# Retention, gated and squared-ReLU feed-forward on one core: where the states are summed, when weight pieces come, and which places stay empty

## The chip, the core and the metric

The kernel runs on one core of one Trainium2 chip. The metric is the device time of one execution in microseconds (us); the median of the runs shown is compared. Engines are named as in the profile: PE (TensorE), DVE (VectorE), ACT (ScalarE), POOL (GpSimd), SP (the queue that issues every DMA here).

## The reference

```
# q, k, v: 4 batches, 8 heads, 576 positions, 64 wide; gamma_h = 1 - 2^(-5-h)
scores = q k^T / sqrt(64)
attn   = (scores * gamma_h^(i-j) where i >= j, else 0) v         # no softmax
x = attn as 2304 tokens x 512
xn = x / rms(x) * rms_g
y = ((silu(xn w_gate) * (xn w_val)) w_out)                        # 512 -> 1536 -> 512
out = (relu(y w_in)^2) w_out2                                     # 512 -> 2048 -> 512
```

All arrays are float32, and so is the result.

## The kernel before, in words

**Precision.** Each float32 operand of the two feed-forward layers is split into a high and a low part that PE takes as fp32r, and every product is three matmuls (high x high, high x low, low x high; `mm3`, L386 to L388). Weights come as 512 KB pieces (`load_piece`, L101, three buffers `st`) and are split on the chip by a "conversion" (`convert_piece`): three ACT instructions (L124, L125, L137) and four on DVE (L126, L129, L132, L138). After a conversion has been put in the program, `load_ahead` puts the load of a later piece into SP's queue; `cv["ahead"]` says how many pieces may be on their way. The load of piece i+3 must wait until piece i's buffer has been read for the last time (L132).

**Attention.** Two heads form a pair; there are 16 pairs, n = 0 to 15. The attention runs in chunks of 128 positions: scores inside a chunk (`scores`, L233), masked by DVE into `ret` (L243, and L251 for the last 64 positions), a running state per chunk (`state`: products k^T v on PE into the PSUM tile `u`, L262; then R by one ACT copy, L269, and a chain of three DVE instructions, L271), and `outputs` (L286 and L294 on PE, scaled by DVE into X, L298). The loop over n does, in this order on PE: `scores(n, 0)`, first place, `outputs(n-1, 0)`, `state(n)`, second place, `scores(n, 1)`, `outputs(n-1, 1)`.

**PSUM.** `bank2("A0")` and `bank2("A1")` are two-bank tiles, one buffer each: the first takes half 0 of a pair's scores (columns 0 to 255 of either bank, one bank a head), the second half 1. Tags "G" and "V" are single banks with two buffers each that go round. Up to pair 7 (`alone["on"]`) the state's `u` comes from "G"; from pair 8 on it comes from "V", which the two outputs of each pair use too, and also the two small matmul groups of the norm (`beside`: "roots", L356, and "scale", L363).

**The places.** From pair 8 on (`mixed`, FIRST = 7) the feed-forward of the first token tile is done beside the attention: 20 blocks (gate or value product of one of 10 column groups, 12 matmuls each) are spread by `block()` over NPOINT = 2 x 9 - SKIP places; with SKIP = 1 only the first place of pair 8 is empty. Each block calls `halves(1)`, and every second half allows one conversion; the end of a mixed pair allows another, and `CONVERT_ALONE` names the pairs before that allow one (2, 3 and 7). `CONVERT_BEHIND` and `cv["phase"]` keep the conversions of some phases behind the last DVE and ACT instructions written before them (phase 2 in pair 8, phase 1, without that, from pair 9).

**The norm.** `NORMS` says behind which half of which pair the squares, the roots, the scaling (L326) and the split into `xh` and `xl` (L373, L374) of a 256-token group stand; these are traced with high priority. Groups 0 and 1 make the first tile (512 tokens), group 2 the second tile (256 tokens), whose split (`split_x(off1[1], T1[1])`) stands behind the first tile's last block.

**Order.** PE and SP keep the order of the program (`manual_schedule`). The order on DVE, ACT and POOL is made by the framework's scheduler, which plays the program through with modelled durations and priorities. Every queue is in order on the chip.

The lines of the state before:

```
u = bank("G" if alone["on"] else "V", f"u{n}")
for c in range(4):
    for h in range(2):
        r = slice(h * D, h * D + D)
        nc.tensor.matmul(u[r, c * D:c * D + D], raw_k[n][:, c, r], vsc[n][:, c, r], start=True, stop=True)
```

Of the kernel before, what the change touches and what calls it, by code (L numbers as in the profile page):

```python
# [22 lines left out]
C = 128  # L23
# [5 lines left out]
T1 = [512, 256, 512, 512, 512]  # L29
# [5 lines left out]
ORDER = [*range(NBESIDE, NF1), *range(NBESIDE)]  # L35
NWA, NWC = NGV + NKEPT // 2, 1
NWB = NF1 - NKEPT // 2 - NWC
SKIP = 1
FIRST = 7
WARM = (8, 6, 5, 5)  # L40
WARM_PAIR = {1: (1, 1), 2: (1, 1)}
NORMS = {
    (4, 0): [("squares", 0)], (4, 1): [("squares", 1)], (5, 0): [("roots", 0)], (5, 1): [("roots", 1)],
    (6, 1): [("scale", 0), ("split", 0)], (7, 0): [("scale", 1), ("split", 1)],
    (9, 1): [("squares", 2)], (11, 0): [("roots", 2)], (12, 0): [("scale", 2)],
}
LOAD_W = (3,)
CONVERT_ALONE = {2: 2, 3: 2, 7: 2}
CONVERT_BEHIND = ("", "", "ad", "ad")
RSQRT_MAGIC = float(0x5F3759DF)  # L50
I32 = mybir.dt.int32
# [5 lines left out]
def retention_then_glu_then_relu2(ctx: ExitStack, tc: tile.TileContext, qk, kv, w1, w2, g, cmask, cvs, cgi, cgc, cid, out):  # L57
# [15 lines left out]
    def bank(tag, name):  # L73
        return psum.tile([P, 512], F32, tag=tag, name=name)

    def bank2(tag, name):
        return psum.tile([P, 2, 512], F32, tag=tag, name=name, bufs=1)
# [18 lines left out]
    def load_piece():  # L96
        i = cv["load"]
        if i >= cv["load_lim"]:
            return
        t = stage.tile([P, 512, 2], I32, tag="st", name=f"raw{i}")  # L100
        nc.sync.dma_start(out=t.rearrange("p n t -> p (n t)"), in_=src[i].bitcast(I32))  # L101
        raws[i] = t
        cv["load"] += 1

    def load_ahead(i):
        while cv["load"] < min(i + cv["ahead"], cv["load_lim"]):
            load_piece()
# [33 lines left out]
    def halves(k):  # L141
        cv["half"] += k
        while cv["half"] >= 2 and convert():
            cv["half"] -= 2
        cv["half"] = min(cv["half"], 2)

    def need(n):
        while cv["done"] < n:
            assert convert()
# [9 lines left out]
    alone = {"on": True}  # L159
    raw_qk, raw_k, vsc, rets, Rs = {}, {}, {}, {}, {}  # L160

    def load_qk(n, parts=(slice(0, S),)):
        if n >= NPAIR:
            return
        if n not in raw_qk:
            b, k = (B - 2 if n % 4 > 1 else B - 1), n % 2 * 2
            raw_qk[n] = ap.tile([P, 2, S], F32, tag="qk", name=f"qk{n}") if n > 9 and n % 4 > 1 else (
                X[:, k:k + 2, b * S:b * S + S]
            )
        for r in parts:  # L170
            nc.sync.dma_start(out=raw_qk[n][:, :, r], in_=qk[n][:, :, r])

    def load_kv(n):
        if n >= NPAIR:
            return
        if n > 1:
            raw_k[n] = kvp.tile([P, 4, P], F32, tag="k", name=f"k{n}")
            vsc[n] = ap.tile([P, 5, P], F32, tag="v", name=f"v{n}", bufs=4)
        else:
            t = X[:, 2 + n, :9 * P].rearrange("p (c n) -> p c n", c=9)  # L180
            raw_k[n], vsc[n] = t[:, :4], t[:, 4:]
        nc.sync.dma_start(out=raw_k[n], in_=kv[n][:, :4])
        nc.sync.dma_start(out=vsc[n], in_=kv[n][:, 4:])
# [5 lines left out]
    ret4 = [ap.tile([P, 2, REM], F32, tag=f"ret4{i}", name=f"ret4_{i}", bufs=1) for i in range(2)]  # L189
    for t in ret4:  # L190
        nc.gpsimd.memset(t[REM:], 0.0)
    junk = {}

    def keep_warm(k, new=False):
        if new:
            junk["t"] = bank("G", f"junk{len(junk)}")
        for _ in range(k):
            nc.tensor.matmul(junk["t"][:, :P], zero, zero, start=True, stop=True)
# [12 lines left out]
        nc.sync.dma_start(out=t, in_=a)  # L211
    for c0, w in ((C, C), (2 * C, REM)):
        nc.gpsimd.tensor_copy(gi[:, :, c0:c0 + w], gi[:, :, :w])
    for n in (2, 3):
        load_qk(n)
        load_kv(n)
        cv["ahead"] += 1
        load_ahead(0)

    def scale_v(n):  # L220
        if n >= NPAIR:
            return
        hp = n % HP
        for h in range(2):
            r = slice(h * D, h * D + D)
            last_on["a"] = nc.scalar.activation(
                out=vsc[n][:, :, r], in_=vsc[n][:, :, r], func=AF.Copy, scale=vs[:, 2 * hp + h:2 * hp + h + 1]
            )

    def score(dst, n, c, h, w):  # L230
        r = slice(h * D, h * D + D)
        cs = slice(c * C, c * C + w)
        nc.tensor.matmul(dst, raw_qk[n][r, 1, cs], raw_qk[n][r, 0, cs], start=True, stop=True)  # L233

    def scores(n, half):
        hp = n % HP
        ps = bank2("A0" if half else "A1", f"s{n}_{half}")
        for j in range(2 + half):
            w = REM if j == 2 else C
            for h in range(2):  # L240
                score(ps[:w, h, j * C:j * C + w], n, 2 * half + j, h, w)
        t = ap.tile([P, 2, 2 * C], F32, tag="ret", name=f"ret{n}_{half}", bufs=3)
        last_on["d"] = nc.vector.tensor_tensor(  # L243
            out=t.rearrange("p h (c i) -> p h c i", c=2),
            in0=ps[:, :, :2 * C].rearrange("p h (c i) -> p h c i", c=2),
            in1=mask[:, 2 * hp:2 * hp + 2, None, :].to_broadcast([P, 2, 2, C]),
            op=ALU.mult,
        )
        rets[n, half] = t
        if half:  # L250
            last_on["d"] = nc.vector.tensor_tensor(  # L251
                out=ret4[n % 2][:REM], in0=ps[:REM, :, 2 * C:2 * C + REM],
                in1=mask[:REM, 2 * hp:2 * hp + 2, :REM], op=ALU.mult,
            )

    def state(n):
        hp = n % HP
        u = bank("G" if alone["on"] else "V", f"u{n}")
        for c in range(4):
            for h in range(2):  # L260
                r = slice(h * D, h * D + D)
                nc.tensor.matmul(  # L262
                    u[r, c * D:c * D + D], raw_k[n][:, c, r], vsc[n][:, c, r],
                    start=True, stop=True,
                )
        if n > 1:
            load_kv(n + 2)
        R = ap.tile([P, 4, D], F32, tag="R", name=f"R{n}")
        last_on["a"] = nc.scalar.activation(out=R[:, 0], in_=u[:, 0:D], func=AF.Copy)  # L269
        for c in range(1, 4):  # L270
            last_on["d"] = nc.vector.scalar_tensor_tensor(  # L271
                out=R[:, c], in0=R[:, c - 1], scalar=gc[:, hp:hp + 1], in1=u[:, c * D:c * D + D],
                op0=ALU.mult, op1=ALU.add,
            )
        Rs[n] = R
# [94 lines left out]
    def split_x(tok, n, col0=0):  # L370
        for k in range(KC):
            src_, d = X[:, k, tok:tok + n], slice(col0, col0 + n)
            last_on["a"] = nc.scalar.activation(out=xh[:, k, d], in_=src_, func=AF.Copy)  # L373
            last_on["d"] = nc.vector.tensor_tensor(out=xl[:, k, d], in0=src_, in1=xh[:, k, d].bitcast(F32), op=ALU.subtract)  # L374


    off1 = [sum(T1[:i]) for i in range(len(T1))]
# [98 lines left out]
    blocks = [(kind, f) for f in range(NBESIDE) for kind in (glu_gate, glu_val)]  # L476
    NPOINT = 2 * (NPAIR - FIRST) - SKIP
    points = {"n": -SKIP, "done": 0}

    def block():  # L480
        points["n"] += 1
        while points["done"] < min(len(blocks), points["n"] * len(blocks) / NPOINT):
            i = points["done"]
            need(i + 1)
            blocks[i][0](0, blocks[i][1], "G")
            points["done"] += 1
            halves(1)

    def stages(n, half):
        with tc.high_priority():  # L490
            for what, i in NORMS.get((n, half), ()):
                beside(what, i)

    for n in range(1, NPAIR + 1):
        mixed = n > FIRST
        if n in LOAD_W:
            cv["ahead"] += 1
            load_ahead(cv["done"])
        if n == FIRST + 1:
            alone["on"] = False  # L500
            cv["phase"] = 2
        if n == FIRST + 2:
            cv["phase"] = 1
        if n < NPAIR:
            scores(n, 0)
        if mixed:
            block()
        else:
            keep_warm(WARM_PAIR.get(n, (0, 0))[0], n in WARM_PAIR)
        outputs(n - 1, 0)  # L510
        stages(n, 0)
        if n < NPAIR:
            state(n)
            if n == NPAIR - 1:
                att_kv.close()
                wpool["c"] = ctx.enter_context(tc.tile_pool(name="wc", bufs=NWC, side="right", reuse_waits="tile"))
                cv["lim"] = NGV + NWC
                cv["load_lim"] = NP1
                load_ahead(cv["done"])
        if mixed:  # L520
            block()
        else:
            keep_warm(WARM_PAIR.get(n, (0, 0))[1])
        if n < NPAIR:
            scores(n, 1)
        outputs(n - 1, 1)
        stages(n, 1)
        scale_v(n + 1)
        halves(CONVERT_ALONE[n] if n in CONVERT_ALONE else 2 * mixed)
    need(NGV)  # L530
# [12 lines left out]
    for f in range(NBESIDE, NF1):  # L543
# [2 lines left out]
        halves(1)  # L546
        glu_val(0, f, "G")
        halves(1)
    split_x(off1[1], T1[1])
    norms = iter(())  # L550
    LAG = 2
    for f in range(NF1 + LAG):
# [161 lines left out]
```

## Time and profile before

| | us |
|---|---|
| median of three runs | 952.05 (947.85 to 953.3) |
| profiled execution | 944.46 |
| its span (first to last instruction) | 942.7 |
| PE busy | 929.0 (99%) |
| DVE busy | 456.4 (48%) |
| ACT busy | 338.6 (36%) |
| granted PE clock, mean | 0.999 |

The attention and what runs beside it fill about the first 150 us; the rest is the feed-forward. A pair's instructions are found in the timeline by their order. A row of a timeline has the start, the time until the last one of the row ends, the engine, the line, the output and inputs, the count, and in brackets the idle time of the engine just before with what ended it.

### The profile page before, as it was taken

What the parts mean: (1) busy time and instruction counts of PE and PEld (TensorE: products, weight loads), DVE (VectorE), ACT (ScalarE), POOL (GpSimd) and SP (SyncE); (2) the same over time, 40 slices, a digit from 0 to 9 for tenths busy, and PEclk for the clock granted to TensorE, in tenths of its full rate; (3) what the DMA queues carried; (4) which work ended last, traced back from release to release, by engine and by line L of the source; (5) the groups of instructions that cost most, each with busy time, mean ns of one, the idle gap of its engine ahead of it and who ended that gap; (6) DMA issues with size and microseconds to landing.
All of it is one profiled execution on the core that took longest, in us unless ns stands there. A gap on an engine that the chain in (4) does not pass through costs nothing.

```text
span 942.7 us, 12628 instructions
## 1 busy us (share of the span) xinstructions
PE 929.0 (99%) x5228; PEld 776.3 (82%) x5228; DVE 456.4 (48%) x859; ACT 338.6 (36%) x606; POOL 22.5 (2%) x56
## 2 busy tenths in 40 slices
PE   9999999999999999999999999999999999999998
PEld 8777777999888888888888888888888888888897
DVE  4987794765644123512677776442223223322322
ACT  3564552652311121112555655432223222322332
POOL 0200000021100000000000000000000000000000
PEclk9999999999999999999999999999999999999999
DMA  9865641410000000100144422001001000100010
GB/s 326 301 218 188 230 162 46 136 44 1 1 1 23 0 1 1 39 7 0 67 134 134 135 89 90 1 5 41 0 1 45 1 1 1 45 1 1 1 46 23
DMA packets 22554, 60.92 MB, mean 65 GB/s; under 512 B 2656, under 2 KB 3936, under 8 KB 22496
## 3 DMA queue, kind: packets, MB, share of 16 engines
q1 hardware_dynamic: 22496, 60.11, 18.8%
q8 instruction: 41, 0.67, 0.3%
q14 instruction: 17, 0.14, 0.0%
HBM read 55.39 MB, written 4.72 MB: 64 GB/s over the span
## 4 chain that ended last, share of the span: by engine, by line
PE 89%; DMA 5%; DVE 3%; ACT 1%; issue 1%; SPq 1%; ACTq 0%
PE pr L388 7%; PE b L628 7%; PE pr L387 7%; PE pr L386 7%; PE b L629 7%; PE b L630 7%; PE a L387 5%; PE a L386 5%; PE a L388 5%; PE pg L386 5%; PE pg L387 5%; PE pg L388 5%; PE pv L386 5%; PE pv L388 5%; PE pv L387 5%; DMA raw<-in_w 4%
## 5 line engine op out<-in xcount | busy, mean ns | idle before, releaser
L617 DVE TENSOR_TENSOR X<-X 128x512 f32<-128x512 f32 (+1 forms) x80 | 51.1, 639 | 189.3 <-ACT X L616 188.6
L415 ACT ACTIVATE h<-X 128x512 fp32r<-128x512 f32 (+1 forms) x132 | 77.5, 587 | 161.7 <-DVE X L434 86.8
L416 DVE TENSOR_TENSOR h<-X,h 128x512 fp32r<-128x512 f32 (+1 forms) x132 | 84.5, 640 | 70.7 <-ACT h L415 69.5
L388 PE MATMUL pr<-xh,w 128*128 128x512 f32 (+1 forms) x320 | 117.7, 368 | 0.0
L387 PE MATMUL pr<-xl,w 128*128 128x512 f32 (+1 forms) x320 | 117.7, 368 | 0.0
L386 PE MATMUL pr<-xh,w 128*128 128x512 f32 (+1 forms) x320 | 117.6, 368 | 0.0
L616 ACT ACTIVATE X<-pr 128x512 f32<-128x512 f32 (+1 forms) x80 | 44.5, 556 | 194.5 <-PE pr L388 194.3
L628 PE MATMUL b<-w,h 128*128 128x512 f32 x288 | 112.4, 390 | 0.0
L629 PE MATMUL b<-w,h 128*128 128x512 f32 x288 | 112.2, 390 | 0.0
L630 PE MATMUL b<-w,h 128*128 128x512 f32 x288 | 112.0, 389 | 0.0
L386 PE MATMUL pv<-xh,w 128*128 128x512 f32 (+1 forms) x240 | 90.5, 377 | 0.0
L387 PE MATMUL pg<-xl,w 128*128 128x512 f32 (+1 forms) x240 | 88.6, 369 | 1.6 <-DVE xl L374 1.6
L386 PE MATMUL pg<-xh,w 128*128 128x512 f32 (+1 forms) x240 | 89.6, 373 | 0.0
L387 PE MATMUL a<-h,w 128*128 128x512 f32 (+1 forms) x240 | 88.5, 369 | 0.0
L386 PE MATMUL a<-h,w 128*128 128x512 f32 (+1 forms) x240 | 88.5, 369 | 0.0
L388 PE MATMUL pv<-xh,w 128*128 128x512 f32 (+1 forms) x240 | 88.4, 368 | 0.0
L388 PE MATMUL pg<-xh,w 128*128 128x512 f32 (+1 forms) x240 | 88.4, 368 | 0.0
L388 PE MATMUL a<-h,w 128*128 128x512 f32 (+1 forms) x240 | 88.4, 368 | 0.0
L387 PE MATMUL pv<-xl,w 128*128 128x512 f32 (+1 forms) x240 | 88.3, 368 | 0.0
L434 DVE TENSOR_TENSOR X<-pv,X 128x512 f32<-128x512 f32 (+1 forms) x52 | 32.7, 628 | 110.9 <-PE pv L388 109.1
L426 ACT ACTIVATE X<-pg 128x512 f32<-128x512 f32 (+1 forms) x52 | 28.5, 549 | 114.0 <-PE pg L388 114.0
L387 PEld LDWEIGHTS pr<-xl,w 128*128 128x128 f32 x320 | 60.3, 188 | 10.7
(93 smaller groups left out, 1412.0 us busy)
## 6 DMA issues: line engine op xcount, KB each, us to landing
raw<-in_w SPq DMA_DIRECT2D x68, 512.0 KB, 3.7
X<-in_qk SPq DMA_DIRECT2D x11, 576.0 KB, 6.2
out<-o SPq DMA_DIRECT2D x18, 256.0 KB, 2.1
v<-in_kv SPq DMA_DIRECT2D x14, 320.0 KB, 4.3
k<-in_kv SPq DMA_DIRECT2D x14, 256.0 KB, 3.1
qk<-in_qk SPq DMA_DIRECT2D x4, 576.0 KB, 4.2
X<-in_kv SPq DMA_DIRECT2D x2, 320.0 KB, 5.3
X<-in_kv SPq DMA_DIRECT2D x2, 256.0 KB, 5.0
```

Source lines behind the costliest of these rows:

```text
L386: nc.tensor.matmul(dst, whi, xhi, start=start, stop=False, skip_group_check=True)
L387: nc.tensor.matmul(dst, whi, xlo, start=False, stop=False, skip_group_check=True)
L388: nc.tensor.matmul(dst, wlo, xhi, start=False, stop=stop, skip_group_check=True)
L415: last_on["a"] = nc.scalar.activation(out=h[:, 0, :n], in_=s, func=AF.Copy)
L416: last_on["d"] = nc.vector.tensor_tensor(out=h[:, 1, :n], in0=s, in1=h[:, 0, :n].bitcast(F32), op=ALU.subtract)
L426: last_on["a"] = nc.scalar.activation(out=s, in_=pg[:, :n], func=AF.Silu)
L434: last_on["d"] = nc.vector.tensor_tensor(out=s, in0=pv[:, :n], in1=s, op=ALU.mult)
L616: last_on["a"] = nc.scalar.activation(out=s, in_=pg[:, :n], func=AF.Relu)
L617: last_on["d"] = nc.vector.tensor_tensor(out=s, in0=s, in1=s, op=ALU.mult)
L628: nc.tensor.matmul(a[m], hh, w[:, 0], start=f == 0, stop=False)
L629: nc.tensor.matmul(a[m], hh, w[:, 1], start=False, stop=False)
L630: nc.tensor.matmul(a[m], hl, w[:, 0], start=False, stop=f == NF2 - 1)
```

## The change

States: when `alone` is off, `state(n)` writes its 256 columns into columns 256 to 511 of the first bank of the pair's own half-0 scores tile (A0), where before it took a bank from "V". Prologue: `LOAD_W` is emptied, and three weight pieces are loaded before the loop, each ahead of the q, k and v of pairs 2 and 3 (the third behind them), where before there were two, each behind them. Pair 1 allows a conversion too. Both places of pair 8 are empty, so 20 blocks are spread over 16 places. Roots and scaling of group 2 stand one half and two halves later. Phase 2 begins with pair 7. The second tile's split is traced with high priority.

```diff
-SKIP = 1
+SKIP = 2
...
-    (9, 1): [("squares", 2)], (11, 0): [("roots", 2)], (12, 0): [("scale", 2)],
+    (9, 1): [("squares", 2)], (11, 1): [("roots", 2)], (13, 0): [("scale", 2)],
...
-LOAD_W = (3,)
-CONVERT_ALONE = {2: 2, 3: 2, 7: 2}
+LOAD_W = ()
+CONVERT_ALONE = {1: 2, 2: 2, 3: 2, 7: 2}
...
-    for n in (2, 3):
-        load_qk(n)
-        load_kv(n)
+    for n in (2, 3, 4):
         cv["ahead"] += 1
         load_ahead(0)
+        if n < 4:
+            load_qk(n)
+            load_kv(n)
...
         rets[n, half] = t
+        if not half:
+            spare_bank[n] = ps[:, 0, 2 * C:]
...
-        u = bank("G" if alone["on"] else "V", f"u{n}")
+        u = bank("G", f"u{n}") if alone["on"] else spare_bank.pop(n)
...
         if n == FIRST + 1:
             alone["on"] = False
+        if n == FIRST:
             cv["phase"] = 2
...
-    split_x(off1[1], T1[1])
+    with tc.high_priority():
+        split_x(off1[1], T1[1])
```

## Rows read from the trace of the kernel before

**Rows 1.** The page's first part: busy us, share of the span, instructions.

```profile
PE 929.0 (99%) x5228; PEld 776.3 (82%) x5228; DVE 456.4 (48%) x859; ACT 338.6 (36%) x606; POOL 22.5 (2%) x56
```

**Rows 2.** Waits of PE, whole span: total us, times, longest.

```profile
PE u L262 <- DVE X L298: 3.8, 3, 2.0
PE ssq L356 <- DVE aside L352: 2.1, 1, 2.1
PE pg L387 <- DVE xl L374: 1.6, 2, 1.2
PE o L286 <- DVE R L271: 1.3, 1, 1.3
```

**Rows 3.** Timeline of PE, 60 to 140 us: start, us, instruction, idle before.

```profile
69.61 0.71 PE L233 MATMUL s<-qk 64*128 64x128 f32 x8
...
89.78 0.69 PE L262 MATMUL u<-v,k 128*64 128x64 f32 x16 [2.01 <-DVE X L298]
...
101.53 0.69 PE L262 MATMUL u<-v,k 128*64 128x64 f32 x16 [0.77 <-DVE X L298]
...
130.24 0.72 PE L233 MATMUL s<-qk 64*128 64x128 f32 x8
...
135.25 0.44 PE L286 MATMUL o<-qk,R 64*64 64x128 f32 x4 [1.32 <-DVE R L271]
```

**Rows 4.** Timeline of DVE, 50 to 136 us.

```profile
51.77 0.68 DVE L243 TENSOR_TENSOR ret<-s,mask 128x512 f32<-128x512 f32 x1
...
73.81 0.27 DVE L271 SCALAR_TENSOR_TENSOR R<-R,gc,u 128x64 f32<-128x64 f32 x1
...
89.30 0.42 DVE L298 TENSOR_TENSOR X<-o,gi 128x256 f32<-128x256 f32 x1
...
101.06 0.42 DVE L298 TENSOR_TENSOR X<-o,gi 128x256 f32<-128x256 f32 x1
...
134.83 0.27 DVE L271 SCALAR_TENSOR_TENSOR R<-R,gc,u 128x64 f32<-128x64 f32 x1
```

**Rows 5.** Timeline of PE, 28 to 52 us.

```profile
28.09 0.64 PE L262 MATMUL u<-v,k 128*64 128x64 f32 x16
...
34.62 0.61 PE L356 MATMUL ssq<-ones,aside 128*128 128x1 f32 x4 [2.10 <-DVE aside L352]
...
51.04 0.69 PE L262 MATMUL u<-v,k 128*64 128x64 f32 x16 [1.04 <-DVE X L298]
```

**Rows 6.** Busy us by stretch, clock, DMA share, GB/s.

```profile
53.30:57.50 4.20, 4.20 (x21) 3.22 (x21) 1.17 (x3) 3.42 (x7) 0.00 (x0) 1.00 0.35 130
...
18.50:34.60 16.10, 14.02 (x230) 11.63 (x230) 15.23 (x38) 9.69 (x19) 0.00 (x0) 1.00 1.01 386
```

**Rows 7.** Timeline of SP's queue, 12 to 25 us.

```profile
12.23 0.33 SPq L101 DMA_DIRECT2D raw<-in_w  x1
...
20.30 0.42 SPq L183 DMA_DIRECT2D v<-in_kv  x1
...
22.39 1.98 SPq L101 DMA_DIRECT2D raw<-in_w  x2
```

**Rows 8.** Timeline of ACT, 26 to 28 us.

```profile
26.41 1.01 ACT L226 ACTIVATE v<-v,vs 128x320 f32<-128x320 f32 x2 [1.57 <-DMA v<-in_kv]
```

**Rows 9.** Timeline of ACT, 246 to 251 us.

```profile
249.94 0.60 ACT L461 ACTIVATE X<-a 128x512 f32<-128x512 f32 x1 [0.90 <-DVE X L463]
```

**Rows 10.** Timeline of DVE, 246 to 251 us.

```profile
249.23 0.68 DVE L463 COPY X<-a 128x512 f32<-128x512 f32 x1
```

**Rows 11.** DVE by line, 50 to 145 us: busy, mean ns, idle before.

```profile
L129 DVE SCALAR_TENSOR_TENSOR raw<-raw 128x512 int32<-128x512 int32 x21 | 14.4, 687 | 2.4 <-ACT raw L125 1.9
...
L126 DVE TENSOR_SCALAR u<-u 128x512 f32<-128x512 f32 x21 | 8.8, 420 | 4.6 <-ACT u L124 4.6
```

**Rows 12.** Timeline of DVE, 161 to 165 us.

```profile
161.51 0.42 DVE L374 TENSOR_TENSOR xl<-X,xh 128x256 fp32r<-128x256 f32 x1
161.84 0.68 DVE L434 TENSOR_TENSOR late<-pv,late 128x512 f32<-128x512 f32 x1
...
163.38 1.09 DVE L374 TENSOR_TENSOR xl<-X,xh 128x256 fp32r<-128x256 f32 x3
```

More of the change, by code (lines that the diff above doesn't have):

```diff
@@ L191, in retention_then_glu_then_relu2 @@
         nc.gpsimd.memset(t[REM:], 0.0)
-    junk = {}
+    junk, spare_bank = {}, {}
     def keep_warm(k, new=False):
```

## The prediction

> **What bounds the kernel now.** I read the page's first part, then the waits of PE, then the timelines of PE and of the engine that each wait names, and last the busy time by stretch. PE is busy for 929.0 of 942.7 us [rows 1], so the time can only move by what PE idles. The reader is to see in the waits that nearly all of this idling is early and named: 3.8 us in front of a state, 2.1 in front of the roots' sums, 1.6 in front of the second tile's first product, 1.3 in front of an output [rows 2], 8.8 us in all. No PE work is added or dropped by the change: 20 blocks, all scores, states and outputs and the warming matmuls stay. So the most that it can win is 8.8 us, 0.9% of the time, and what it can lose is new idling of PE.
>
> The sum is made against the profiled execution, 944.46 us with a span of 942.7. That execution lies 7.6 us under the median of the runs shown (952.05) and under their lowest (947.85). I work out a difference and put it on the median.
>
> **The states' new home.** The three waits of a state are 1.04 us in pair 8 [rows 5], 2.01 in pair 11 and 0.77 in pair 12 [rows 3].
>
> In pairs 11 and 12 the state waits for X of the same pair's first output: it ends at 89.72 and 101.48, and the states start at 89.78 and 101.53 [rows 3, 4]. That is so because the norm's small matmuls take a "V" bank between that output and the state, so that the state gets the bank of the output just written. With the states out of "V" and the norm moved half a pair or more, two consecutive owners of a "V" bank are a whole pair's half apart. Both waits go: -2.8 us. If something else in DVE's queue is as late, nothing is gained: 0.
>
> What comes in place are two new orders. First, the state's tile now has another reader. ACT stood idle 0.90 us until 249.94 for a DVE copy that ended at 249.91; the two read different columns of one PSUM tile [rows 9, 10]. So two engines get at a PSUM tile in turn, whatever the columns, and `state(n)` will wait for `ret(n, 0)` (L243), which reads the scores of the same tile. The Trainium skill, PSUM — Partial Sum Buffer, section "PSUM bank collisions raise a hardware error", says the same of one bank: "Semaphore-guard PSUM by bank × quadrant (by bank is the simple version), not by address", and with this the trace agrees (0.90 us of waiting in turn). By it the sum below stands; by addresses alone the state of pair 8 would not wait, and the sum would be 2.4 us lower.
>
> In pair 8 this `ret` ran from 51.77 to 52.45, behind the first tile's scaling and split, while the state started at 51.04 after 1.04 of idling [rows 4, 5]. DVE was full there, and nothing of the change takes work from it between the scaling and that `ret`. The state would start at 52.45: the wait is 2.4 us where it was 1.0, **+1.4 us**. Bounds: -1.0 (the state need not wait at all) and +1.4. I take +1.4. What is queued behind the state on PE is all of pair 8, with no block to fill it now; but PE's total of work is the same, so the blocks moved to later pairs cost nothing themselves.
>
> Second, `scores(n+1, 0)` now writes the tile that R(n) is still read out of, so it waits for the last of the three L271. Before, only `outputs(n, 0)` behind one more place asked for R(n), and that cost 1.32 us once, in front of pair 14's output at 135.25 [rows 3]. By the order of before the new wait would be 4.47 us in pair 10 (R of pair 9 ends at 73.81 + 0.27 = 74.08, the scores started at 69.61) and 4.86 in pair 15 (135.10 against 130.24) [rows 3, 4]. Together 9.3 us: that is the upper bound; the lower is none, with the old 1.32 gone too. Two things shorten it. One conversion more is done before pair 8: 0.42 + 3 x 0.68 = 2.5 us of DVE (the two 128x512 forms not shown take as long as L129) [rows 11]. And pieces 3 to 5 are loaded early, so that DVE should not stand idle again for 4.20 - 1.17 = 3.0 us while a piece comes [rows 6]. For pair 10 that is 5.5 us against 4.47: no wait. For pair 15 only the conversion counts: 4.86 - 2.5 = 2.4. Against the 1.32 that go: **+1.1 us**, bounds -1.3 and +8.0.
>
> **The prologue.** SP's queue now has piece 0 ahead of pair 2, piece 1 ahead of pair 3 and piece 2 behind it. The conversion in pair 1 puts piece 3 into the queue before k and v of pair 4. Before, pieces 2 and 3 were issued at 22.39, behind that v at 20.30; piece 0 at 12.23 [rows 7]. The DMA engines are full from 18.5 to 34.6 at 386 GB/s [rows 6], so 512 KB cost 1.36 us and the v of pair 4 comes 2.7 us later: ACT begins to scale it at 26.41 + 2.7 = 29.1, takes 1.0 [rows 8], and the state of pair 4 can start at 30.1 where it started at 28.09 [rows 5]: +2.0 us of waiting. v of pairs 2 and 3 move by one piece; that wait would be part of the same 2.0, as all hang on one stream of bytes.
>
> On the other side stands the wait of 2.10 us at 34.62, which ends a stretch in which DVE was busy 15.23 of 16.10 us [rows 5, 6]. There DVE is the later one, and it had three conversions in it; now piece 0 is there earlier than its neighbours' loads, and its conversion begins before that stretch. If PE comes 2.0 us later and DVE not, the wait falls to 0.1. So the new wait takes the place of the old, **0 us**; bounds -2.1 (v comes in time after all, and DVE earlier) and +2.0 (DVE as late as PE).
>
> Phase 2 in pair 7 holds the fourth conversion behind that pair's DVE and ACT work. In 43 to 53 us no conversion stood in DVE's queue before, so this keeps that stretch as it was: 0.
>
> **The second tile's split.** Its first subtraction ran at 161.51; then came a product for the output layer and two steps of a conversion, and the other three ran from 163.38 [rows 12]. With priority they follow each other: their inputs are copied by ACT while the first runs. Of the 1.6 us of waiting [rows 2] I take 1.3 as gone; the last 0.3 stay because `xh` and `xl` are still read by the last block. **-1.3 us**, bounds -1.6 and 0. What is pushed back (a value product and a conversion) is wanted two steps later.
>
> **Sum.** -2.8 + 1.4 + 1.1 + 0 - 1.3 = -1.6 us: 942.9 for a profiled execution like this one, and 950.4 on the median.
>
> **Rivals.**
>
> 1. *All named waits go.* DVE has caught up by pair 8, `ret` and R are ready when PE asks, and the prologue's earlier conversion removes the wait at 34.62. For it: DVE is only 48% busy over the span [rows 1], and it idled while a piece came [rows 6]. Against it: full stretches on DVE [rows 6] and DMA are just where the waits lie. Gain 8.8 us: 943.2. With half of it the time would be about 947.
>
> 2. *Slower: the states' chain in A0 decides.* The one-buffer tile is held from the first score until the last L271. If DVE runs as late behind PE as before, the 9.3 us of pairs 10 and 15 come in full. Then: -2.8 + 1.4 + 9.3 - 1.3 (the output's wait, which they contain) - 1.3 (the split) = +5.3, 957.4. It decides from the point where the last R of a pair ends later than a place, the second scores and the second output behind its state. For it: in pairs 9 and 14 R ended 4.5 and 4.9 us too late for this [rows 3, 4]. Against it: a waiting PE lets DVE catch up, and both lags had reasons that the change partly takes away.
>
> 3. *The loads cost without return.* v of pair 4 late by 2.0 us, and the wait at 34.62 stays, as a DVE that waits for later scores is late too: +2.0 on the sum, 952.4.
>
> 4. *The state doesn't wait for `ret`* (the framework tells columns apart): -1.6 - 2.4 = -4.0, 948.0. Against it stands the wait in turn of [rows 9].
>
> **Chances.** Forecast 0.50, rival 1 (or most of it) 0.26, rival 2 0.13, rival 3 0.07, rival 4 0.04. About 0.5% (4.8 us) is what a measurement of this kernel can tell from no change. The forecast, rivals 3 and 4 and a weak form of rival 1 lie within: 0.56 for no change; faster 0.29 (rival 1 and a little of rival 4); slower 0.15 (rival 2 and a tail of rival 3). The range that holds 8 in 10 runs from 943.5 (nearly all of rival 1) to 957.0 (most of rival 2); the likeliest case alone has 947.5 to 953.5.
>
> **What would show it.** Right, if in the profile after: no wait of a state for X is left; the state of pair 8 waits about 2.4 us for `ret` L243; scores L233 wait for R L271 somewhere between pairs 9 and 15, some 2 us in all; a state of pair 4 waits near 28 us for v's scaling by ACT and the wait of L356 is near nothing; and L387 waits for `xl` 0.3 us at most. The prediction is wrong if PE's waits in the first 165 us sum to under 5 us (then rival 1, or the state is free of `ret`), or to over 13 us (then rival 2), or if PE waits in a place that is not named here, such as a block for a piece of weights.

## The result, and the profile after

The changed kernel takes 957.07 us (median of 8, 955.31 to 959.63) against 950.23 for the kernel before (median of 8): ratio 1.0074, 95% interval 1.0048 to 1.0100. It is slower, by 6.8 us; I had forecast a gain of 1.6 us (950.4, from a base of 952.05) and a range up to 957.0. The profiled execution took 957.59 us, with a span of 955.8. One execution of a later run (b_skip2) took 1153.66 us at a mean clock of 0.752 and is left out of that run's ratio.

A note on names: in the code, `scores` takes `bank2("A1")` for half 0 and `bank2("A0")` for half 1. Where the text ahead, the expectations and the headings below say A0, the tile of half 0 is meant.

The first lines of the page after (busy us, share, instructions; and the granted clock in 40 slices):

```profile
PE 937.1 (98%) x5228; PEld 782.8 (82%) x5228; DVE 458.1 (48%) x859; ACT 337.2 (35%) x606; POOL 24.9 (3%) x56
...
PEclk9989989999999999999999999999999999999999
```

Against [rows 1] the same 5228 matmuls are busy 8.1 us longer, and PE idles 955.8 - 937.1 = 18.7 us where it idled 13.7. So of the 13.1 us between the two profiled executions 5.0 are waiting and 8.1 are a slower PE. The second number is a pair of extremes: this execution has the lowest mean clock of the eight (0.989; the others 0.991 to 0.995), and the one before had 0.999. The waits of PE after, to be laid beside [rows 2]:

```profile
PE s L234 <- issue: 4.3, 2, 3.2
PE s L265 <- DVE ret L244: 3.8, 1, 3.8
PE pg L390 <- DVE xl L377: 1.6, 2, 1.3
PE u L265 <- ACT v L227: 1.3, 1, 1.3
...
PE pg L389 <- ACT X L429: 0.7, 1, 0.7
PE pg L389 <- ACT kept L429: 0.7, 1, 0.7
```

No state waits for X any more, and nothing waits at the roots' sums. In their place the state of pair 8, now in tile `s`, waits 3.8 us for `ret`, and scores wait 4.3 us. Blocks wait twice for ACT to empty a bank (L389, 0.7 us each), a place that the prediction does not name. "issue" there means that the profile names no releaser; the timelines of PE and then of DVE show whom they waited for:

```profile
20.59 1.13 PE L265 MATMUL u<-v,k 128*64 128x64 f32 x16 [1.33 <-ACT v L227]
...
56.70 1.12 PE L265 MATMUL s<-v,k 128*64 128x64 f32 x16 [3.81 <-DVE ret L244]
...
77.00 0.72 PE L234 MATMUL s<-qk 64*128 64x128 f32 x8 [1.14 <-issue]
...
124.90 0.71 PE L234 MATMUL s<-qk 64*128 64x128 f32 x8 [0.44 <-ACT w L137]
...
138.26 1.23 PE L234 MATMUL s<-qk 64*128 64x128 f32 x8 [3.19 <-issue]
...
175.99 0.39 PE L390 MATMUL pg<-xl,w 128*128 128x256 f32 x1 [1.25 <-DVE xl L377]
```

```profile
54.84 0.41 DVE L126 TENSOR_SCALAR u<-u 128x512 f32<-128x512 f32 x1
55.17 0.68 DVE L129 SCALAR_TENSOR_TENSOR raw<-raw 128x512 int32<-128x512 int32 x1
55.77 0.27 DVE L274 SCALAR_TENSOR_TENSOR R<-R,gc,u 128x64 f32<-128x64 f32 x1
55.96 0.68 DVE L244 TENSOR_TENSOR ret<-s,mask 128x512 f32<-128x512 f32 x1
...
76.31 0.60 DVE L274 SCALAR_TENSOR_TENSOR R<-R,gc,s 128x64 f32<-128x64 f32 x2
...
123.88 0.91 DVE L274 SCALAR_TENSOR_TENSOR R<-R,gc,s 128x64 f32<-128x64 f32 x3
...
137.89 0.27 DVE L274 SCALAR_TENSOR_TENSOR R<-R,gc,s 128x64 f32<-128x64 f32 x1
```

The last R of pairs 9, 13 and 14 ends at 76.91, 124.79 and 138.16; the scores of the next pair start at 77.00, 124.90 and 138.26. The order is the one foretold, scores behind the last R. The wait of 0.44 us, which the profile puts down to ACT, is one of them, so that scores wait 4.8 us in all. The stretches (busy us of PE, PEld, DVE, ACT, POOL with counts, then clock, DMA share, GB/s) show the rest:

```profile
21.00:28.00 7.00, 6.96 (x66) 5.65 (x66) 5.55 (x13) 4.39 (x9) 0.00 (x0) 0.55 1.02 381
...
55.00:62.00 7.00, 5.30 (x54) 4.73 (x56) 5.85 (x15) 2.85 (x7) 0.00 (x0) 0.56 0.42 141
...
137.00:144.00 7.00, 5.74 (x19) 4.58 (x20) 6.53 (x13) 3.03 (x5) 0.00 (x0) 0.56 0.51 156
```

```profile
120.00:140.00 20.00, 16.37 (x152) 12.89 (x151) 19.88 (x45) 12.63 (x24) 0.00 (x0) 0.95 0.60 198
```

Behind each of the three longest waits (1.33, 3.81, 3.19 us) PE runs some 7 us at a granted clock of about half (0.55 and 0.56 in these stretches), 1.2 GHz instead of 2.4; behind the wait of 1.14 us it does not (1.00 from 77 to 84 us). From 120 to 140 us DVE is full (19.88 of 20 us), while the scores of pair 15 wait for it.

### The profile page after: what moved, and what is told of

The parts are those of the page before. It is cut to its first block, busy times and chain, and to the rows that moved or that the text cites. A ratio compares the mean times of both kernels' runs of the same rounds, so it can differ in the third digit from the quotient of the medians.

```text
span 955.8 us, 12627 instructions
## 1 busy us (share of the span) xinstructions
PE 937.1 (98%) x5228; PEld 782.8 (82%) x5228; DVE 458.1 (48%) x859; ACT 337.2 (35%) x606; POOL 24.9 (3%) x56
## 3 DMA queue, kind: packets, MB, share of 16 engines
q1 hardware_dynamic: 22496, 60.11, 18.7%
## 4 chain that ended last, share of the span: by engine, by line
PE 92%; DMA 4%; ACT 2%; DVE 1%; issue 1%; SPq 1%; ACTq 0%
PE pr L390 7%; PE b L633 7%; PE pr L391 7%; PE pr L389 7%; PE b L634 7%; PE b L635 7%; PE a L390 5%; PE a L389 5%; PE a L391 5%; PE pv L389 5%; PE pg L389 5%; PE pv L391 5%; PE pv L390 5%; PE pg L390 5%; PE pg L391 5%; DMA raw<-in_w 2%
## 5 line engine op out<-in xcount | busy, mean ns | idle before, releaser
L389 PE MATMUL pr<-xh,w 128*128 128x512 f32 (+1 forms) x320 | 117.6, 368 | 0.0
L389 PE MATMUL pv<-xh,w 128*128 128x512 f32 (+1 forms) x240 | 91.5, 381 | 0.0
L389 PE MATMUL pg<-xh,w 128*128 128x512 f32 (+1 forms) x240 | 89.6, 373 | 1.4 <-ACT X L429 0.7
L389 PE MATMUL a<-h,w 128*128 128x512 f32 (+1 forms) x240 | 88.5, 369 | 0.0
L389 PEld LDWEIGHTS pr<-xh,w 128*128 128x128 f32 x320 | 60.3, 188 | 10.8
```

The lines of the kernel that those rows point to most:

```text
L389: nc.tensor.matmul(dst, whi, xhi, start=start, stop=False, skip_group_check=True)
```

## The experiments

Ratios are against the kernel before, run on the same chip beside them; each run has 6 or 12 executions, and intervals are 95%. Chips differ between the experiments, so ratios are compared and not times. "Junk" matmuls compute nothing that is used; they keep PE busy.

**States back in "V", all else as changed.**

```diff
-u = bank("G", f"u{n}") if alone["on"] else spare_bank.pop(n)
+u = bank("G" if alone["on"] else "V", f"u{n}")
```

> The changed kernel with its states back in a bank of V, all else as changed. Theory 1 (states in A0 make PE wait, and the granted clock falls behind each long wait): the waits for ret (3.81 us) and of scores for R (4.8 us) go, an old-style wait of about 1 us in pair 8 returns, and two of the three stretches at half clock (about 3.2 us of time each) go: 957 - 8.6 + 2 - 6.4 = about 944 to 947. Rival (the two empty places and the fuller ones behind them, or the prologue, cost the time): 955 to 958.

Measured: 952.70 us, 1.0033 (1.0017 to 1.0050), better than the change but not as expected. The waits for `ret` and of scores are gone, but the scaling's bank of pair 13 now stands between an output and the state:

```profile
120.46 1.12 PE L265 MATMUL u<-v,k 128*64 128x64 f32 x16 [4.25 <-DVE X L301]
```

**The prologue as before, all else as changed.**

```diff
-LOAD_W = ()                              # and the loop over (2, 3, 4), loads ahead of q, k, v
-CONVERT_ALONE = {1: 2, 2: 2, 3: 2, 7: 2}
+LOAD_W = (3,)
+CONVERT_ALONE = {2: 2, 3: 2, 7: 2}
```

> The changed kernel with the prologue's loads, LOAD_W and the conversions before pair 8 as before. Theory 1: the state of pair 2 no longer waits 1.33 us for v, the clock stays at 2.4 GHz from 20 to 30 us (3.2 us), the wait of 2.1 us at the roots' sums returns: 957 - 1.3 - 3.2 + 2.1 = about 954.5. A rival by which the prologue carries most of the loss: 950 or lower. A rival by which the extra conversion helped DVE later: pairs 9 to 15 wait longer and the time is 958 or more.

Measured: 959.43 us, 1.0095 (1.0071 to 1.0119). The prologue is no cause of the loss; without it scores wait 5.6 us where they waited 4.3:

```profile
PE s L233 <- issue: 5.6, 3, 4.1
```

The interval overlaps that of the whole change (1.0048 to 1.0100), so that its gain here is not shown.

**The states' tile alone, on the kernel before.**

```diff
+if not half: spare_bank[n] = ps[:, 0, 2 * C:]
-u = bank("G" if alone["on"] else "V", f"u{n}")
+u = bank("G", f"u{n}") if alone["on"] else spare_bank.pop(n)
```

> The kernel before with its states in A0 and nothing else. Theory 1: the state of pair 8 waits for ret about 2 us or more (1.0 before), scores wait for R in pairs 10 and 15 by 2 to 9 us, the clock falls behind the long ones, and the 2.8 us of pairs 11 and 12 go: 952 to 960, slower. Rival (only together with both places of pair 8 empty does it cost time): 947 to 950.

Measured: 961.41 us, 1.0117 (1.0091 to 1.0142): by itself this part costs the whole loss (the intervals overlap a little, so that more than that is not shown). Its waits of PE, and two rows each of PE's and DVE's timeline:

```profile
PE s L233 <- issue: 8.4, 2, 4.3
PE s L264 <- DVE ret L243: 2.5, 1, 2.5
```

```profile
80.53 1.23 PE L233 MATMUL s<-qk 64*128 64x128 f32 x8 [4.33 <-issue]
...
146.30 1.23 PE L233 MATMUL s<-qk 64*128 64x128 f32 x8 [4.06 <-issue]
```

```profile
80.17 0.26 DVE L273 SCALAR_TENSOR_TENSOR R<-R,gc,s 128x64 f32<-128x64 f32 x1
...
145.93 0.27 DVE L273 SCALAR_TENSOR_TENSOR R<-R,gc,s 128x64 f32<-128x64 f32 x1
```

The reader is to see that the bound read from the trace of before (4.47 and 4.86 us) comes nearly in full, in the same pairs (the last R of pairs 9 and 14 ends at 80.43 and 146.20), and that the state of pair 8 waits the 2.4 us worked out for it. A third wait, 1.20 us in pair 14, makes 9.6 us of scores waiting in all.

**Junk matmuls where PE waits, in the changed kernel.**

```diff
-WARM_PAIR = {1: (1, 1), 2: (1, 1)}
+WARM_PAIR = {1: (1, 1), 2: (7, 1)}
         outputs(n - 1, 0)
+        if n == FIRST + 1:
+            keep_warm(15, True)
```

> The changed kernel with junk matmuls put where PE waits: six more ahead of the outputs in the first place of pair 2, and 15 (some 3.7 us) behind the first outputs of pair 8. The waits stay as long, only filled. Theory 1: the clock stays at 2.4 GHz behind both, 6 to 7 us less: about 950.5. Rival (the loss is the waits alone, and the clock in the profile belongs to that execution): no change, 956 to 958, or longer by what the junk adds.

Measured: 956.62 us, 1.0062 (1.0040 to 1.0084): hardly less than the change (1.0074), and within the intervals. The half clock from 21 to 28 us and from 55 to 62 is gone from the profile (a shorter one came, 0.57 from 62 to 66 us), but other waits came:

```profile
PE s L234 <- ACT u L124: 4.3, 1, 4.3
PE s L234 <- issue: 3.0, 2, 2.6
...
PE s L265 <- DVE ret L244: 1.3, 1, 1.3
```

The wait of 4.3 us is pair 15's: its scores started at 138.01 here and at 138.26 in the changed kernel. The last R of pair 14 ends at 137.90 in this run. A PE that is faster before only comes earlier to the same moment, which DVE sets.

**The state copied out of A0 by ACT, all else as changed.**

```diff
         R = ap.tile([P, 4, D], F32, tag="R", name=f"R{n}")
+        if not alone["on"]:
+            ps_u, u = u, ap.tile([P, 4 * D], F32, tag="us", name=f"us{n}", bufs=1)
+            last_on["a"] = nc.scalar.activation(out=u, in_=ps_u[:, :4 * D], func=AF.Copy)
```

> The changed kernel, but in pairs 8 to 15 ACT copies the whole state out of the scores' tile (one 128x256 copy, about 0.4 us) and R is made from the copy, so that A0 is free after one ACT instruction and not after the last of three on DVE. Theory 1 (scores wait because R, late in DVE's full queue, holds A0): the waits of scores (1.14, 0.44 and 3.19 us) fall under 1 us in all and the stretch at half clock behind the last (138 to 145 us) goes: 957 - 4 - 3.3 = about 950 to 952. Rival (PE is only as early as DVE's and ACT's conversions let it be, so the wait moves to the outputs that read R or to a block): the outputs wait 2 to 4 us instead, 955 to 957.

Measured: 949.94 us, 1.0012 (0.9994 to 1.0030). From 1.0074 to 1.0012 are 0.6%, most of the loss, although eight ACT copies were added; the interval reaches 1. Its waits of PE:

```profile
PE s L265 <- DVE ret L244: 3.4, 1, 3.4
PE pg L392 <- ACT kept L432: 3.4, 1, 3.4
...
PE s L234 <- DMA X<-in_qk: 0.7, 1, 0.7
```

No score waits for R any more. The scores of pair 15 on PE, and the last R of pair 14 on DVE:

```profile
135.21 0.71 PE L234 MATMUL s<-qk 64*128 64x128 f32 x8
```

```profile
137.96 0.27 DVE L277 SCALAR_TENSOR_TENSOR R<-R,gc,us 128x64 f32<-128x64 f32 x1
```

That R is as late as in the changed kernel (137.89); the scores, at 138.26 there, now start 2.75 us ahead of it. What counts is who holds the tile meanwhile. The half clock behind the old wait is gone with it (1.00 from 138 to 145 us).

**Three parts alone on the kernel before:** the prologue; roots and scaling of group 2 at (11, 1) and (13, 0); SKIP = 2.

```diff
# b_prologue
-LOAD_W = (3,)                            # and the loads of three pieces as in the change
+LOAD_W = ()
+CONVERT_ALONE = {1: 2, 2: 2, 3: 2, 7: 2}
# b_norms
+(11, 1): [("roots", 2)], (13, 0): [("scale", 2)],
# b_skip2
+SKIP = 2
```

> The kernel before with the loads of the prologue, LOAD_W and the conversion in pair 1 as changed, and nothing else. Theory 1: a wait of 0.3 to 1.3 us for v in pair 2, the 2.1 us in front of the roots' sums nearly gone with the half clock that follows them in some executions: 2 to 4 us faster, 946 to 948. Rival (earlier weights delay the attention's inputs): 951 to 953.

> The kernel before with roots and scaling of group 2 at (11, 1) and (13, 0), and nothing else. If the state still takes its bank from V, the scaling's bank stands between an output and the state of pair 13 now: the waits of 2.01 and 0.77 us go and one of 2 to 4 us comes in pair 13 (4.25 us in the kernel with states in V and all else changed): 950 to 953. Rival (the later place is better in itself): 946 to 948.

> The kernel before with both places of pair 8 empty, and nothing else. Theory 1: the wait of the state in pair 8 stays about 1 to 1.7 us, PE reaches the next blocks 5.7 us of work earlier while DVE is full, so a block or a state waits 1 to 3 us for DVE: 951 to 954. Rival (no effect, as PE's work is the same): 949 to 951.

Measured: 947.62 us, 0.9987 (0.9972 to 1.0002); 948.88 us, 1.0003 (0.9985 to 1.0021); 950.70 us, 1.0024 (1.0003 to 1.0045). The prologue is at most a small gain, less than expected; the norm's place moves a wait (now one of 2.79 us in pair 13, first row below) and no time; the empty place costs about 0.2%, with an interval that nearly reaches 1. None of the three explains the loss. Phase 2 in pair 7 was not run alone.

```profile
113.84 0.69 PE L262 MATMUL u<-v,k 128*64 128x64 f32 x16 [2.79 <-DVE X L298]
```

The second of them shows something else, from 36 to 40 us, right behind its wait of 2.10 us at the roots' sums, first in this run and then in the profiled execution of the kernel before, where the same wait is as long [rows 5]:

```profile
36.00:40.00 4.00, 4.00 (x50) 3.57 (x52) 3.48 (x11) 1.74 (x5) 2.26 (x8) 0.57 0.52 172
```

```profile
36.00:40.00 4.00, 4.00 (x62) 3.44 (x62) 3.86 (x13) 1.68 (x5) 2.84 (x11) 1.00 0.72 222
```

So the same wait is followed by half clock in one execution and not in another. Among the 35 executions of the kernel before that ran beside these, the shortest had 944.73 us at a mean clock of 0.999, the longest 952.14 at 0.992; their median clock is 0.995. The profile that I worked from was one of those that kept the clock.

**The state of pair 8 in "G"; the same with the copy; with SKIP = 1 besides; and these two with the prologue alone on the kernel before.**

```diff
# a_g8
+u = bank("G", f"u{n}") if alone["on"] or n == FIRST + 1 else spare_bank.pop(n)
# a_g8_copy: besides, the ACT copy above for n > FIRST + 1
# a_g8_copy_skip1: besides
+SKIP = 1
# b_pro_g8_copy: the kernel before with the prologue, the line of a_g8 and the copy
```

> The changed kernel with the state of pair 8 in a bank of G (free there, as both places of pair 8 are empty), the states of pairs 9 to 15 in A0 as changed. The wait for ret (3.81 us) goes. If waits simply add up: 3.8 us and the half clock behind it (3.2 us) less, 950. If PE only comes earlier to the scores that wait for R (as with the junk matmuls, where 3.2 us of half clock went and the time fell by 0.5): 955 to 957, with 4 to 7 us of waiting in front of scores.

> As the last, and with the state copied out of A0 by ACT from pair 9 on: both new waits of the change are gone. Against the copy alone (949.9): if the wait for ret was worth its length, 3.4 us and some clock less, 944 to 947, below the kernel before; if the wait for ACT in front of a gate block (3.39 us there) takes it up, 949 to 950.

> As the last, with blocks in the second place of pair 8 again (SKIP = 1). If the empty place costs time because PE then comes too early to blocks whose bank ACT has not emptied: 1 to 3 us less than the last. If not: the same within 1 us.

> The kernel before with three parts only: the prologue as changed, states of pairs 9 to 15 in A0 and copied out by ACT, the state of pair 8 in G. Norm, SKIP and phases as before. The waits of a state for X (3.8 us) go and the 2.1 us at the roots' sums fall under 0.7: 942 to 946, faster than before. Rival (DVE's and ACT's conversions hold PE anyway): 946 to 949.

Measured: 956.87 us, 1.0091 (1.0071 to 1.0112); 947.58 us, 0.9998 (0.9985 to 1.0011); 947.95 us, 1.0000 (0.9981 to 1.0019); 948.66 us, 1.0003 (0.9989 to 1.0016). The waits of PE in the first:

```profile
PE s L234 <- issue: 6.6, 3, 4.1
PE o L289 <- DVE R L274: 3.3, 2, 2.6
```

Taking the wait for `ret` away alone gave nothing: the second output of pair 7 waits for R in its place (3.3 us), and the scores wait longer. With both holds gone the loss is gone. That all three versions with the copy end at the kernel before, and none under it, was not expected. In the last two (a_g8_copy_skip1, b_pro_g8_copy) pair 8 has a block in its second place again, and the trace shows it waiting for a bank of "G":

```profile
55.84 0.60 PE L392 MATMUL pg<-xh,w 128*128 128x512 f32 x1 [4.36 <-DVE R L277]
```

```profile
55.71 0.77 PE L392 MATMUL pg<-xh,w 128*128 128x512 f32 x1 [2.97 <-DVE R L277]
```

The state of pair 8 now has one of the two "G" banks and, by the order of the code, pair 7's R is read out of the other. So there the hold came back in another tag, which may be why these two won nothing. In the second of these four PE still waits in pair 8, behind the first tile's norm and split on DVE, which end at 52.57:

```profile
PE o L292 <- DVE R L277: 3.3, 2, 2.6
```

**Half clock where no scores wait for R; and before's own wait filled.**

```diff
# a_g8_copy_warm: a_g8_copy, in pair 8 behind the second scores
+if n == FIRST + 1: keep_warm(14, True)
# b_warm5: the kernel before
+WARM_PAIR = {1: (1, 1), 2: (1, 1), 5: (8, 0)}
```

> The changed kernel with the state of pair 8 in G, the later states copied out of A0, and 14 junk matmuls (about 3.4 us) ahead of pair 8's second outputs, where PE waited 3.3 us for R and ran at half clock from 56 to 62 us afterwards. If half clock is time of its own where no engine behind PE holds it up: 3.4 us less than without the junk, 944 to 945. Rival (as with the junk in the changed kernel, PE only comes earlier to another wait): 946 to 948.

> The kernel before with eight junk matmuls (about 2 us) in the first place of pair 5, where PE waits 2.1 us for the squares in front of the roots' sums. The profiled execution of before kept its full clock through that wait, others of the same kernel have a mean clock of 0.992 to 0.996. If the spread of before's times (944.7 to 952.1) is this wait's clock: a median of 945 to 947 and a spread of half. Rival (the spread comes from elsewhere): 948 to 950, spread as before.

Measured: 951.55 us, 1.0029 (1.0012 to 1.0046), and 947.43 us, 0.9978 (0.9956 to 1.0000). The first failed as an experiment: the junk itself waited for a bank of "G" that R was being read from, and the clock fell all the same (0.50 from 56 to 60 us).

```profile
57.12 3.15 PE L198 MATMUL junk<-xl 128*128 128x128 f32 x13 [4.50 <-DVE R L277]
```

The second filled the wait:

```profile
PE ssq L356 <- DVE aside L352: 0.2, 1, 0.2
```

Its 12 executions lie between 946.09 and 950.34, the 23 of before beside them between 944.62 and 954.46 (standard deviations 1.2 and 2.7 us); the spread is halved, as expected if that wait's clock makes much of it. The gain of 0.2% touches no change at the end of its interval.

## Why the prediction was wrong, point by point

**R holds the scores' tile: the step that failed.** The mechanism was named, and its upper bound (9.3 us) was right: 8.4 us in the same two pairs when this part stands alone (9.6 with pair 14). I discounted it to 2.4 us of new waiting by crediting DVE with one conversion less and with no idling in 53 to 57 us. In the changed kernel it was 1.14 + 0.44 + 3.19 = 4.8 us against 1.3 before: +3.5 where I had +1.1. The larger credit was misread, and the smaller was used up before pair 15.

The 3.0 us for pair 10 were misread. Of the two idle times of DVE in 53 to 57 us before, only the first ends with a conversion's step, the second with PE's value product:

```profile
54.79 0.69 DVE L129 SCALAR_TENSOR_TENSOR raw<-raw 128x512 int32<-128x512 int32 x1 [1.49 <-ACT raw L125]
...
57.50 0.69 DVE L434 TENSOR_TENSOR kept<-pv,kept 128x512 f32<-128x512 f32 x1 [1.51 <-PE pv L388]
```

And DVE did idle again for pieces, between 62 and 70 us, behind ACT, which waited for them. ACT's row first, then two of DVE's:

```profile
61.60 0.66 ACT L124 ACTIVATE u<-raw 128x512 f32<-128x512 f32 x1 [2.91 <-DMA raw<-in_w]
```

```profile
62.30 0.43 DVE L126 TENSOR_SCALAR u<-u 128x512 f32<-128x512 f32 x1 [1.37 <-ACT u L124]
...
69.58 0.69 DVE L129 SCALAR_TENSOR_TENSOR raw<-raw 128x512 int32<-128x512 int32 x1 [1.14 <-ACT raw L125]
```

The credit of one conversion was used up by pair 14. Counted in the traces, DVE had done 32 steps of conversions before the last R of pair 9 and 35 in the changed kernel; before the last R of pair 14 it had done 88 in both. From 120 to 140 us DVE was full in the changed kernel. So pair 15 waited 3.19 us and not 2.4; why it was not the full 4.86 no run singles out.

The copy shows what the hold was worth: 0.6% of the time, nearly the whole loss. Rival 2 was this very mechanism, at 957.4; I gave it 0.13. That its time agrees with the measured one is partly luck: it has 9.3 us of waiting scores where 4.8 came, no clock, and a base 1.8 us above the median that was measured.

**No term for the clock.** The sum had only waits. In the profiled execution three waits were followed by some 21 us at half clock, and PE was busy 8.1 us longer: more than any term I wrote. Much of that is chance: the mean clocks of these two executions differ by 0.010, the medians by 0.002, and a wait of 2.1 us was followed by half clock in one execution and not in another. An estimate for the medians: over the 104 executions of the kernel before that ran beside the experiments, 0.001 of mean clock goes with 0.8 us, where the median clock is 0.995; it is 0.993 in the eight of the changed kernel. That makes some 1.5 of the 6.8 us clock, which with the 5.0 us of waiting is about the loss. It is no measurement: the junk matmuls took two of the three stretches away for about 0.1%, within the intervals, because DVE set the next moment anyway; the run meant to settle it (a_g8_copy_warm) did not, and no other was made.

**The base.** I put the difference of a profiled execution on the median. That execution had kept its full clock (0.999, and the row from 36 to 40 us above). Four in five of those 104 executions have a mean clock of 0.996 or less, so the usual one seems to have a stretch at half clock too, and its median lies higher than the profile's waits explain. Where that stretch lies was seen only in b_norms.

**State of pair 8: right in kind, 1.4 us short.** 2.4 us were worked out, 2.48 came when the states moved alone, 3.81 in the whole change. Two instructions of the fourth conversion ran just ahead of `ret` (54.84 and 55.17, about 1 us). Phase 2 in pair 7, which I put at nothing, holds them behind pair 7's last instructions, but `ret` is written later and they came in between. Yet this wait had little price of its own: without it (a_g8) the time was no shorter, as an output waited 3.3 us in its place.

That the state waits for `ret` at all I had read from [rows 9, 10]. There the two reads lie in two banks of one tile (m = 2 and 3 in `acc_of`); a row just behind them, where the two lie in one bank, has the same wait. So accesses are put in turn by tile here, one bank or two:

```profile
251.44 0.66 ACT L461 ACTIVATE X<-a 128x256 f32<-128x256 f32 x2 [0.90 <-DVE X L463]
```

**The states' waits for X: right.** All 3.8 us are gone. (In pairs 11 and 12 that X is the one of the pair before, `outputs(n - 1, 0)`, and not of the same pair, as I wrote.) But the move of the norm by itself only shifts them (2.79 us in pair 13, b_norms; 4.25 in a_states_in_v), which I had not seen.

**The prologue: right on balance.** The wait at the sums went, and a wait for v came, in pair 2 (1.33 us) and not in pair 4. In the profiled execution half clock followed it. By itself the part measures 0.9987, its interval just including 1.

**The split's priority: wrong.** 1.6 us before, 1.6 after; the same product and conversion still run between the first subtraction and the others. Compiled with and without the priority, every engine has the same sequence of instructions, so this part changes nothing at all. Why the scheduler places them alike is not shown; it may have had nothing else ready. I had taken a word of the program for an order of the queue.

## What to carry to other kernels

Whoever moves a result into unused columns of another tile takes over that tile's whole life: here the next scores had to wait for the slowest reader of the state, at the end of a chain on the fullest engine. Price such a hold at the lag that the trace already shows, and do not take it down for relief elsewhere unless that relief reaches the same moment; or free the tile by one early copy. And where the profiled execution kept the full clock through its waits, look at the clock of other executions before adding a wait to it.

## What the runs showed of the hardware that was not expected

In the changed kernel's profiled execution a wait of PE of 1.33 us was followed by about 7 us at about half clock (0.55 from 21 to 28 us), and one of 1.14 us by none. In the kernel before, one of 2.10 us was followed by none in the profiled execution, while in another run (b_norms) the same wait was followed by a clock of 0.57 from 36 to 40 us. Thirty-five executions of the kernel before, beside one another, spread by 7.4 us (944.73 at a mean clock of 0.999 to 952.14 at 0.992); time and mean clock go together there with a correlation of -0.88.
